# Half-row products and a PSUM bank per head in a windowed attention with two expert layers

## The chip, the cores and the metric

The kernel runs on one core of a Trainium2 chip. The metric is the device time of one execution in microseconds (us). The engines are PE (TensorE: matrix products and transposes), DVE (VectorE), ACT (ScalarE), POOL (GpSimd) and SP (SyncE, which only issues DMA transfers). Each works through its own queue in program order and waits for the others by semaphores. A matrix product reads both operands from SBUF, with the summed index along the partitions, and writes one of eight banks of PSUM, each 128 partitions of 512 fp32 numbers; DVE and ACT read PSUM, POOL doesn't.

## The reference

Attention over 4 batches, 8 heads, 576 positions and 64 numbers per head comes first. Heads 0 to 3 ("plain") see a window of 32 positions, heads 4 to 7 ("dilated") every fourth position of the last 128. Its output, 2304 rows of 512 numbers, passes a layer of eight experts with one chosen per row and a skip score, and then a gated layer.

```
scores = (q @ k.T) / sqrt(64)              # per batch and head, 576 x 576
rel    = i - j
plain:   0 <= rel < 32                     # heads 0..3
dilated: 0 <= rel < 128 and rel % 4 == 0   # heads 4..7
attn   = exp(where(mask, scores, -1e9) - max); attn /= sum + 1e-9
x      = attn @ v                          # -> 2304 x 512
rows with x @ w_skip > 0: x += p * (relu(x @ w1[e]) @ w2[e]),  e = argmax(x @ w_gate), p its softmax weight
out    = (sigmoid(x @ w_gate2) * (x @ w_val)) @ w_out
```

## The kernel before, in words

**Tiles.** The attention is cut into 40 tiles (batch, kind, j): four batches, plain (kind 0) and dilated (kind 1), and five tiles of up to 128 positions (the last plain tile has 64). A batch and kind are a unit of five tiles with four heads. The dilated heads sort their positions by the remainder modulo 4, so that a dilated tile, too, has four groups c of 32 positions with a window of 64 keys each. In a tile a head has the number 2m + h2. K and V hold the two heads h2 of a pair m one above the other: h2 = 0 in partitions 0 to 63, h2 = 1 in 64 to 127.

**Zero blocks.** `kT` keeps, for each pair, one block of columns per head; the half of the partitions that belongs to the other head is zero there. A product over all 128 partitions with q of both heads thus gives each head's scores in its own columns. `vp` and `vd`, the values with windows of 64 keys in 64 partitions per head, have zero blocks in the same way; `vp` has a 65th column of ones, which sums the weights. All zeros are written once, in `setup` (L78) and `clear_dil` (L118): L100 and L101 on DVE, L102 to L104 and L114 to L116 on POOL, L123 on ACT. The same function writes the masks, small bf16 copies on DVE (L105 to L111).

**The work on a tile.** `stage_s` (L244) lays the mask (0 or -1e30) into a bank with one product by the identity (L248) and adds the scores by eight products of 32 queries and 2 x 64 columns, each on one of four groups of 32 columns of PE (`tile_position`, L260); DVE takes the maximum (L265). `stage_e` subtracts it (DVE, L272) and takes the exponential (ACT, L274). `stage_pt` turns the weights (PE, L286) and copies them (L291 or L289). `stage_pv` multiplies by the values in eight products of 130 or 128 columns (L307, L312). `stage_z`, `stage_z1`, `stage_r` and `stage_x` make the sum (L326, dilated tiles only), add 1e-9 (L334), take the reciprocal (L338) and scale (L358), all on DVE; `stage_x` stores the result by one or four DMAs.

**PSUM.** Scores have two banks (`ps_s`), turned weights one (`ps_p`), outputs two (`ps_o`), transposes and logits two (`ps_t`), routing one (`ps_r`); a tile of scores or outputs fills one bank.

**The order of a step.** `attention_phase` (L448) writes the order by hand. Step s issues the scores of tile s, the exponential of s, the turning of s-1, the values of s-2 and the scaling of s-3. `take` puts in the transposes of q and k for the next unit (`tr_plain` L209, `tr_dil` L226), whose PSUM results ACT copies (L242; some of the first on DVE, L240), and releases loads of later q and k. `stage_gate` turns finished rows of x (L383), and `stage_logits` (eight products on 32 columns each, L417, K of 128) and L428 make the routing logits a step later. `todo` places the routing of a batch and `shift_v` (L189: copies each window's second half of V to its first half's partitions; on DVE for the first unit, else on POOL). `keep_busy` issues products that nothing reads (L1619). Loads of the experts' weights (L918) go out on SP between those of V. After the loop the last three tiles are finished, the routing ends, and the expert layer and the gated layer follow; none of those is changed.

The order of one step, as the loop writes it:

```
att.stage_s(*tiles[s])
if s >= 3: att.stage_z(*tiles[s - 3])
run(s, 0, 1); take()            # logits of a gate; a transpose
att.stage_e()
if s >= 3: att.stage_z1()
run(s, 0)
att.stage_pt(*tiles[s - 1])
if s >= 3: att.stage_r(); att.stage_x(*tiles[s - 3])
att.stage_pv(*tiles[s - 2])
```

Of the kernel before, what the change touches and what calls it, by code (L numbers as in the profile page):

```python
# [28 lines left out]
class Attention:  # L29
# [6 lines left out]

    def __init__(self, nc, tc, ctx, g, q, k, v, w_skip, w_gate, xd):
# [40 lines left out]
    def setup(self):  # L78
# [45 lines left out]

    def setup_late(self):
        self.clear_dil(1)
# [29 lines left out]
    def load_v(self, b, kind, between=None):  # L156

        nc = self.nc
        for m in range(2):
            for h2 in range(2):  # L160
                src = self.v[b, 4 * kind + 2 * m + h2]
                p1 = 64 * h2 + W
                if kind == 0:
                    nc.sync.dma_start(
                        out=self.vp[p1:p1 + W, 0:18, m, h2, 0:D],
                        in_=src.rearrange("(c p) d -> p c d", p=W),
                    )
                else:
                    vv = self.vd[:, :, m, h2].rearrange("p j r d -> p j (r d)")
# [9 lines left out]
    def shift_v(self, kind, m, h2, eng):  # L179

        p0, p1 = 64 * h2, 64 * h2 + W
        if kind == 0:
            to, of = self.vp[p0:p1, 1:18, m, h2, 0:D], self.vp[p1:p1 + W, 0:17, m, h2, 0:D]
        else:
            to, of = (
                t.rearrange("p j r d -> p j (r d)")
                for t in (self.vd[p0:p1, 1:5, m, h2], self.vd[p1:p1 + W, 0:4, m, h2])
            )
# [15 lines left out]
    def tr_plain(self, b, nm, c):  # L204
# [6 lines left out]
        for h2 in range(2):  # L211
            for jj in range(2):
# [3 lines left out]
                else:  # L216
                    dst = self.kT[0][64 * h2:64 * h2 + 64, :, h2, W + lo + jj:W + hi:2]
                self.evac(dst, src)

    def tr_dil(self, b, nm, c, m):  # L220
# [7 lines left out]
        for h2 in range(2):  # L228
            for jj in range(2):
# [3 lines left out]
                else:  # L233
                    dst = self.kT[1][64 * h2:64 * h2 + 64, m, h2, jj:4:2, W + lo:W + hi]
# [8 lines left out]

    def stage_s(self, b, kind, j):  # L244
        nc = self.nc
        s = self.bank(self.ps_s, "s", "ps_s", 4, 2 * W)
        mask = self.masks[0 if j else 1 + kind]
        nc.tensor.matmul(  # L248
            s.rearrange("p h t -> p (h t)"), lhsT=self.identb, rhs=mask.rearrange("p h t -> p (h t)"),
            start=True, stop=False, skip_group_check=True,  # L250
        )
        for m in range(2):
            for c in range(2 if (j == 4 and kind == 0) else 4):
                if kind == 0:
                    t0 = 128 * j + W * c
                    lhsT, rhs = self.qT[0][:, m, t0:t0 + W], self.kT[0][:, m, :, t0:t0 + 2 * W]
                else:
                    t0 = W * j
                    lhsT, rhs = self.qT[1][:, m, c, t0:t0 + W], self.kT[1][:, m, :, c, t0:t0 + 2 * W]
                nc.tensor.matmul(  # L260
# [187 lines left out]
def attention_phase(att, route, extra):  # L448
# [47 lines left out]
    for s in range(n):  # L496
# [8 lines left out]
        if s >= 3:  # L505
            att.stage_z(*tiles[s - 3])
# [4 lines left out]
        if s >= 3:  # L511
            att.stage_z1()
# [1193 lines left out]
```

## Time and profile before

| | us |
|---|---|
| three runs | 778.4, 781.0, 784.0 |
| median | 781.0 |
| the profiled execution | 783.2 |
| its span, first to last instruction | 781.5 |
| PE busy | 733.2 (94%) |
| DVE busy | 419.9 (54%) |
| ACT busy | 306.9 (39%) |
| POOL busy | 141.3 (18%) |

The busy shares are those of the span. An engine is busy while it executes; the time in which it waits or issues a transfer is not counted. Ends of PE's products are modelled, and a following product begins before the one ahead of it ends. The timeline merges instructions of a line that follow one another: start, duration, engine, line, operation, tiles, shape, count, and in brackets the idle time before it and what ended it. An fp32 product appears as two instructions.

### The profile page before, as it was taken

The numbers are of one execution on the slowest core, as the hardware profiler recorded it, in microseconds if no ns is written. First come the engines' busy times: TensorE is split into PE (matmuls) and PEld (weight loads), VectorE is DVE, ScalarE is ACT, GpSimd is POOL, SyncE is SP. The second block draws the span as 40 slices with busy tenths as digits, with TensorE's granted clock in tenths as the row PEclk, the third lists the DMA queues.
The fourth block names the chain that finished last, engine by engine and source line by source line (L and its number), as shares of the span: only waits on it lengthen the run. The fifth ranks groups of instructions, "written<-read, shape, count | busy, mean of one in ns | idle before, by whom it ended". The sixth has DMA issues, their size and how long they took to land.

```text
span 781.5 us, 13025 instructions
## 1 busy us (share of the span) xinstructions
PE 733.2 (94%) x4976; PEld 594.7 (76%) x4976; DVE 419.9 (54%) x880; ACT 306.9 (39%) x677; POOL 141.3 (18%) x163
## 2 busy tenths in 40 slices
PE   5999988779999779999999999999999999999995
PEld 3666665568988778978888888888888888888884
DVE  8767767556777757332234546534652653332332
ACT  4888884234545544333352323313321331111110
POOL 7224332312343233100011002000110010000000
PEclk9999999899999989999999999999999999999999
DMA  8799879595597762321012103100310000000122
GB/s 151 166 211 218 226 168 309 162 348 199 184 332 255 264 231 65 117 81 55 1 32 76 28 27 96 40 27 22 87 28 27 28 1 0 1 1 27 55 81 85
DMA packets 74997, 88.12 MB, mean 113 GB/s; under 512 B 15810, under 2 KB 52930, under 8 KB 74912
## 3 DMA queue, kind: packets, MB, share of 16 engines
q1 hardware_dynamic: 71008, 78.68, 34.9%
q0 software_dynamic: 2560, 6.15, 2.2%
q10 hardware_dynamic: 1344, 2.10, 0.7%
q8 instruction: 60, 0.98, 0.5%
q14 instruction: 25, 0.20, 0.1%
HBM read 75.52 MB, written 13.63 MB: 114 GB/s over the span
## 4 chain that ended last, share of the span: by engine, by line
PE 78%; DVE 7%; ACT 6%; DMA 5%; issue 3%; POOL 0%; SPq 0%; DVEq 0%; ACTq 0%; POOLq 0%
PE bank L942 26%; PE bank L947 13%; PE bank L935 8%; PE bank L933 8%; PE bank L934 8%; PE bank L1165 6%; DMA cv_raw<-in_moe_w_val_dram 2%; DMA cv_raw<-in_moe_w_gate_dram 2%; DVE w_lo L928 1%; ACT qTd L242 1%; PE ps_s L260 1%; ACT kTp L242 1%; ACT kTd L242 1%; PE ps_t L383 1%; DVE hl L1211 1%
## 5 line engine op out<-in xcount | busy, mean ns | idle before, releaser
L942 PE MATMUL bank<-fxh,w_hi 128*128 128x512 f32 (+1 forms) x480 | 177.7, 376 | 0.7 <-ACT fxh L1333 0.7
L942 PE MATMUL bank<-fxh,w_lo 128*128 128x512 f32 (+1 forms) x480 | 174.7, 370 | 0.0
L1359 DVE SCALAR_TENSOR_TENSOR th<-th,bank 128x512 f32<-128x512 f32 (+1 forms) x60 | 38.0, 634 | 184.3 <-PE bank L947 161.8
L947 PE MATMUL bank<-fxl,w_hi 128*128 128x512 f32 (+1 forms) x480 | 121.2, 372 | 0.0
L942 PEld LDWEIGHTS bank<-fxh,w_hi 128*128 128x128 f32 x480 | 90.3, 188 | 19.7 <-ACT fxh L1333 1.3
L1007 POOL TENSOR_TENSOR cv_x<-cv_x,cv_s 128x512 f32<-128x512 f32 x36 | 47.6, 1326 | 307.5 <-DVE cv_x L1046 282.2
L942 PEld LDWEIGHTS bank<-fxh,w_lo 128*128 128x128 f32 x480 | 90.3, 188 | 16.1
L947 PEld LDWEIGHTS bank<-fxl,w_hi 128*128 128x128 f32 x480 | 85.6, 188 | 17.5
L1165 PE MATMUL bank<-xt,w 128*128 128x128 f32 (+3 forms) x512 | 74.6, 309 | 16.6 <-issue 9.4
L1360 ACT CAST gh<-th 128x512 fp32r<-128x512 f32 (+1 forms) x60 | 34.7, 578 | 135.3 <-DVE th L1359 135.3
L1165 PEld LDWEIGHTS bank<-xt,w 128*128 128x128 f32 x512 | 71.8, 210 | 19.4 <-issue 9.6
L933 PE MATMUL bank<-w_hi,gh 128*128 128x512 f32 x216 | 85.6, 396 | 0.0
L934 PE MATMUL bank<-w_lo,gh 128*128 128x512 f32 x216 | 85.2, 395 | 0.0
L935 PE MATMUL bank<-w_hi,gl 128*128 128x512 f32 x216 | 85.2, 394 | 0.0
L1358 ACT ACTIVATE th<-bank 128x512 f32<-128x512 f32 (+1 forms) x60 | 33.3, 555 | 127.3 <-PE bank L947 126.8
L1375 DVE SCALAR_TENSOR_TENSOR fo<-bank,fo 128x512 f32<-128x512 f32 x90 | 61.6, 687 | 5.1 <-PE bank L935 3.0
L1361 DVE TENSOR_TENSOR gl<-th,gh 128x512 fp32r<-128x512 f32 (+1 forms) x60 | 39.2, 653 | 38.6 <-ACT gh L1360 38.6
L935 PEld LDWEIGHTS bank<-w_hi,gl 128*128 128x128 f32 x216 | 40.5, 188 | 9.6
L933 PEld LDWEIGHTS bank<-w_hi,gh 128*128 128x128 f32 x216 | 40.7, 188 | 9.2
L934 PEld LDWEIGHTS bank<-w_lo,gh 128*128 128x128 f32 x216 | 40.6, 188 | 9.1
L1002 ACT ACTIVATE cv_x<-cv_raw 128x512 f32<-128x512 f32 x36 | 24.2, 674 | 57.4 <-issue 32.8
L928 DVE TENSOR_TENSOR w_lo<-w,w_hi 128x1024 fp32r<-128x1024 f32 x32 | 41.3, 1292 | 3.7 <-ACT w_hi L927 3.4
(215 smaller groups left out, 1052.8 us busy)
## 6 DMA issues: line engine op xcount, KB each, us to landing
w<-in_moe_w_dram SPq DMA_DIRECT2D x62, 512.0 KB, 6.7
cv_raw<-in_moe_w_val_dram SPq DMA_DIRECT2D x12, 512.0 KB
cv_raw<-in_moe_w_out_dram SPq DMA_DIRECT2D x12, 512.0 KB, 7.1
cv_raw<-in_moe_w_gate_dram SPq DMA_DIRECT2D x10, 512.0 KB, 3.9
out_dram<-fo SPq DMA_DIRECT2D x18, 256.0 KB, 2.0
fx<-xd SPq DMA_DIRECT2D x16, 256.0 KB, 3.0
kp<-in_k_dram SPq DMA_DIRECT2D x12, 192.0 KB, 4.1
qp<-in_q_dram SPq DMA_DIRECT2D x12, 192.0 KB, 5.2
```

What stands on the lines that cost most here:

```text
L928: self.nc.vector.tensor_tensor(out=lo, in0=raw, in1=hi.bitcast(F32), op=ALU.subtract)
L933: nc.tensor.matmul(out, lhsT=lh[0], rhs=rh[0], start=first, stop=False)
L934: nc.tensor.matmul(out, lhsT=lh[0], rhs=rh[1], start=False, stop=False)
L935: nc.tensor.matmul(out, lhsT=lh[1], rhs=rh[0], start=False, stop=last)
L942: nc.tensor.matmul(out, lhsT=lh[a][:, k], rhs=rh[0][:, k], start=first and k + a == k0, stop=False, skip_group_check=True,)
L947: nc.tensor.matmul(out, lhsT=lh[0][:, k], rhs=rh[1][:, k], start=False, stop=last and k == k1 - 1, skip_group_check=True)
L1007: nc.gpsimd.tensor_tensor(out=self.x[i], in0=self.x[i], in1=self.s.pop(i), op=ALU.mult)
L1165: nc.tensor.matmul(ps[:, a, 0:n], lhsT=wt.one[4 * e + c][:, k, 128 * a:128 * a + 128], rhs=xt[:, k, 0:n], start=(k == 0), stop=(k == 3),)
L1359: nc.vector.scalar_tensor_tensor(out=th, in0=th, scalar=1.0, in1=ps[1], op0=ALU.add, op1=ALU.mult)
L1360: nc.scalar.copy(out=hi, in_=th)
L1361: nc.vector.tensor_tensor(out=lo, in0=th, in1=hi.bitcast(F32), op=ALU.subtract)
L1375: nc.vector.scalar_tensor_tensor(out=o, in0=ps, scalar=0.5, in1=o, op0=ALU.mult, op1=ALU.add)
```

## The change

Each product of scores or values now uses only the 64 partitions of its head, on the upper or lower half of PE's rows, and writes a PSUM bank of its head, since both halves may write at one time. K and V lose the zero blocks, and the instructions that wrote them go. Scores and outputs fill two banks each and keep one buffer (`ps_s`, `ps_o`). The mask takes one product per bank. The sum, reciprocal and scaling of tile s-3 move ahead of the scores of tile s. At the end of the attention the scaling of the third last tile comes earlier, and some banks are borrowed from other pools. The reads on DVE get a fourth dimension of access, with the same numbers of elements.

```diff
-        self.ps_s = pool("ps_s", 2, space=PSUM)
+        self.ps_s = pool("ps_s", 1, space=PSUM)
...
-        self.ps_o = pool("ps_o", 2, space=PSUM)
+        self.ps_o = pool("ps_o", 1, space=PSUM)
...
-            big.tile([128, 2, 2, W + S], F32, name="kTp"),
-            big.tile([128, 2, 2, 4, W + 160], F32, name="kTd"),
-        )
-        self.vp = big.tile([128, 18, 2, 2, D + 1], F32, name="vp")
-        self.vd = big.tile([128, NJ, 2, 2, 4, D], F32, name="vd")
+            big.tile([128, 2, W + S], F32, name="kTp"),
+            big.tile([128, 2, 4, W + 160], F32, name="kTd"),
+        )
+        self.vp = big.tile([128, 18, 2, D + 1], F32, name="vp")
+        self.vd = big.tile([128, NJ, 2, 4, D], F32, name="vd")
...
-        self.clear_dil(0)
+        ve.memset(self.kT[0][:, :, 0:W], 0.0)
+        ve.memset(self.vp[:, :, :, D:D + 1], 1.0)
         for h2 in range(2):
-            lo, hi = 64 * h2, 64 * h2 + 64
-            ve.memset(self.kT[0][lo:hi, :, 1 - h2], 0.0)
-            ve.memset(self.kT[0][lo:hi, :, h2, 0:W], 0.0)
-            gp.memset(self.vp[lo:lo + W, 0:1, :, h2, 0:D], 0.0)
-            gp.memset(self.vp[lo:hi, :, :, 1 - h2], 0.0)
-            gp.memset(self.vp[lo:hi, :, :, h2, D:D + 1], 1.0)
+            gp.memset(self.vp[64 * h2:64 * h2 + W, 0:1, :, 0:D], 0.0)
...
-            gp.memset(self.vd[lo:lo + W, 0:1, :, h2], 0.0)
-            gp.memset(self.vd[lo + W:hi, 4:5, :, h2], 0.0)
-            gp.memset(self.vd[lo:hi, :, :, 1 - h2], 0.0)
-
-    def clear_dil(self, h2):
-        lo, hi = 64 * h2, 64 * h2 + 64
+            gp.memset(self.vd[lo:lo + W, 0:1], 0.0)
+            gp.memset(self.vd[lo + W:hi, 4:5], 0.0)
         for m in range(2):
-            k = self.kT[1][lo:hi, m]
-            for block in (k[:, 1 - h2], k[:, h2, :, 0:W], k[:, h2, :, W + 144:]):
-                self.nc.scalar.copy(out=block, in_=self.zero[lo:hi].unsqueeze(2).to_broadcast(list(block.shape)))
+            k = self.kT[1][:, m]
+            for block in (k[:, :, 0:W], k[:, :, W + 144:]):
+                self.nc.scalar.copy(out=block, in_=self.zero.unsqueeze(2).to_broadcast(list(block.shape)))
 
     def setup_late(self):
-        self.clear_dil(1)
...
+    def heads(self, pool, tag, name, n):
+
+        t = pool.tile([128, 2, 512], F32, tag=tag, name=name)
+        return t[:, :, 0:2 * n].rearrange("p h (m t) -> p h m t", m=2)
...
-        s = self.bank(self.ps_s, "s", "ps_s", 4, 2 * W)
+        s = self.heads(self.ps_s, "s", "ps_s", 2 * W)
         mask = self.masks[0 if j else 1 + kind]
-        nc.tensor.matmul(
-            s.rearrange("p h t -> p (h t)"), lhsT=self.identb, rhs=mask.rearrange("p h t -> p (h t)"),
-            start=True, stop=False, skip_group_check=True,
-        )
+        for h2 in range(2):
+            nc.tensor.matmul(
+                s[:, h2], lhsT=self.identb, rhs=mask[:, 0:2], start=True, stop=False, skip_group_check=True
+            )
         for m in range(2):
             for c in range(2 if (j == 4 and kind == 0) else 4):
...
+                for h2 in range(2):
+                    p = slice(64 * h2, 64 * h2 + 64)
+                    if kind == 0:
+                        t0 = 128 * j + W * c
+                        lhsT, rhs = self.qT[0][p, m, t0:t0 + W], self.kT[0][p, m, t0:t0 + 2 * W]
...
+                    nc.tensor.matmul(
+                        s[32 * c:32 * c + 32, h2, m], lhsT=lhsT, rhs=rhs,
+                        start=False, stop=True, skip_group_check=True, tile_position=(64 * h2, 32 * c),
+                    )
...
+                for h2 in range(2):
+                    p = slice(64 * h2, 64 * h2 + 64)
+                    oc = o[32 * c:32 * c + 32, h2, m]
+                    if kind == 0:
+                        rhs = self.vp[p, 4 * j + c, m]
+                    else:
+                        oc, rhs = oc[:, 0:D], self.vd[p, j, m, c]
                     nc.tensor.matmul(
-                        oc, lhsT=lhsT, rhs=self.vp[:, 4 * j + c, m], start=True, stop=True,
-                        skip_group_check=True, tile_position=(0, 32 * c),
+                        oc, lhsT=pt[p, m, 32 * c:32 * c + 32], rhs=rhs, start=True, stop=True,
+                        skip_group_check=True, tile_position=(64 * h2, 32 * c),
                     )
...
-        att.stage_s(*tiles[s])
         if s >= 3:
             att.stage_z(*tiles[s - 3])
+            att.stage_z1()
+            att.stage_r()
+            att.stage_x(*tiles[s - 3])
+        att.stage_s(*tiles[s])
         run(s, 0, 1)
...
         att.stage_e()
-        if s >= 3:
-            att.stage_z1()
...
-        if s >= 3:
-            att.stage_r()
-            att.stage_x(*tiles[s - 3])
-            if tiles[s - 3][1] == 1:
-                gates.append(tiles[s - 3][::2])
+        if s >= 3 and tiles[s - 3][1] == 1:
+            gates.append(tiles[s - 3][::2])
...
-    att.stage_pv(*last[1])
+    x(last[0])
+    att.stage_pv(*last[1], (att.ps_s, "s", "ps_s"))
...
-    att.stage_pv(*last[2], (att.ps_p, "pt", "ps_p"))
+    att.stage_pv(*last[2])
```

## Rows read from the trace of the kernel before

**Rows 1.** Stages: us; busy (count) of PE, PEld, DVE, ACT, POOL; clock; DMA, GB/s

```profile
24.32:132.66 108.34, 99.40 (x1678) 67.76 (x1677) 79.58 (x294) 86.64 (x288) 37.60 (x61) 0.98 0.89 213
...
150.00:182.00 32.00, 24.71 (x157) 22.68 (x158) 15.08 (x18) 11.23 (x16) 6.66 (x7) 0.89 0.94 318
182.00:781.00 599.00, 579.87 (x2874) 486.43 (x2873) 292.97 (x464) 191.60 (x324) 78.73 (x62) 0.99 0.24 80
```

**Rows 2.** The same view, cut into steps: 8, 12, 15, 35, 37, 38

```profile
37.53:40.73 3.20, 2.68 (x45) 1.72 (x44) 1.99 (x7) 3.06 (x10) 0.00 (x0) 1.00 1.07 178
...
49.76:52.64 2.88, 2.88 (x55) 2.19 (x55) 2.17 (x9) 2.32 (x9) 0.00 (x0) 1.00 0.52 128
...
58.65:60.95 2.30, 2.30 (x46) 1.61 (x44) 1.40 (x7) 2.18 (x9) 1.04 (x1) 1.00 0.95 258
...
119.23:120.97 1.74, 1.74 (x37) 1.05 (x36) 1.48 (x6) 0.25 (x1) 0.77 (x1) 1.00 1.15 274
...
122.82:126.93 4.11, 2.31 (x44) 1.27 (x42) 3.87 (x15) 1.48 (x5) 2.33 (x4) 0.95 1.03 287
126.93:129.88 2.95, 2.95 (x41) 1.57 (x38) 1.79 (x9) 0.38 (x2) 1.71 (x8) 0.50 0.98 310
```

**Rows 3.** Timeline of DVE, 0 to 15 us

```profile
1.43 1.07 DVE L100 MEMSET kTp<- 64x1216 f32 x1 [0.20 <-issue]
...
4.58 3.00 DVE L107 COPY mask<-mask 32x256 bf16<-32x256 bf16 x3
...
10.62 1.40 DVE L240 COPY qTp<-ps_t 64x192 f32<-64x192 f32 x4
...
14.44 0.43 DVE L265 TENSOR_REDUCE mx<-ps_s 128x4 f32<-128x256 f32 x1
```

**Rows 4.** Timeline of POOL, 0 to 16 us

```profile
4.67 2.06 POOL L103 MEMSET vp<- 64x2340 f32 x1
...
6.97 0.54 POOL L114 MEMSET vd<- 32x512 f32 x1
```

**Rows 5.** Timeline of PE, 0 to 26 us

```profile
5.14 0.85 PE L209 MATMUL ps_t<-ident,qp 96*128 96x96 f32 x4
6.77 1.01 PE L1619 MATMUL ps_t<-r_one 128*128 128x512 bf16 x2 [0.78 <-ACT kTp L242]
...
12.07 1.08 PE L260 MATMUL ps_s<-kTp,qTp 128*32 128x128 f32 x16 [3.25 <-DVE qTp L240]
```

**Rows 6.** Timeline of SP, then DMA issues with KB and us to landing

```profile
3.85 4.11 SPq L164 DMA_DIRECT2D vp<-in_v_dram  x4
...
vp<-in_v_dram SPq DMA_DIRECT2D x4, 144.0 KB, 5.8
```

**Rows 7.** Timeline of PE in step 12

```profile
49.76 0.27 PE L248 MATMUL ps_s<-mask,identb 128*128 128x256 bf16 x1
49.96 0.65 PE L260 MATMUL ps_s<-kTp,qTp 128*32 128x128 f32 x16
50.42 0.40 PE L417 MATMUL ps_l<-xt,w 128*32 128x128 f32 x8
...
51.12 0.65 PE L307 MATMUL ps_o<-vp,pt 128*32 128x130 f32 x16
51.71 0.66 PE L383 MATMUL ps_t<-ident,x 128*128 128x128 f32 x4
```

**Rows 8.** Timeline of PE, logits of the last tiles

```profile
138.13 0.43 PE L417 MATMUL ps_l<-xt,w 128*32 128x128 f32 x8
...
138.81 0.32 PE L417 MATMUL ps_l<-xt,w 128*32 128x64 f32 x8
```

**Rows 9.** Timeline of DVE in step 12

```profile
50.67 0.42 DVE L265 TENSOR_REDUCE mx<-ps_s 128x4 f32<-128x256 f32 x1 [0.56 <-PE ps_s L260]
...
51.34 0.41 DVE L272 TENSOR_TENSOR sb<-ps_s,mx 128x256 f32<-128x256 f32 x1
...
52.27 0.42 DVE L358 TENSOR_TENSOR x<-ps_o,z 128x256 f32<-128x256 f32 x1
```

More of the change, by code (lines that the diff above doesn't have):

```diff
@@ L182, in shift_v @@
         if kind == 0:
[L183 removed]
+            to, of = self.vp[p0:p1, 1:18, m, 0:D], self.vp[p1:p1 + W, 0:17, m, 0:D]
         else:
@@ L186, in shift_v @@
                 t.rearrange("p j r d -> p j (r d)")
-                for t in (self.vd[p0:p1, 1:5, m, h2], self.vd[p1:p1 + W, 0:4, m, h2])
+                for t in (self.vd[p0:p1, 1:5, m], self.vd[p1:p1 + W, 0:4, m])
             )
@@ L252, in stage_s @@
         for m in range(2):
             for c in range(2 if (j == 4 and kind == 0) else 4):
[L254 to L260, printed above, removed]
-                    s[32 * c:32 * c + 32, 2 * m:2 * m + 2, :], lhsT=lhsT, rhs=rhs,
-                    start=False, stop=True, skip_group_check=True, tile_position=(0, 32 * c),
-                )
+                for h2 in range(2):
[4 more added lines that the diff above has]
+                    else:
+                        t0 = W * j
+                        lhsT, rhs = self.qT[1][p, m, c, t0:t0 + W], self.kT[1][p, m, c, t0:t0 + 2 * W]
+                    nc.tensor.matmul(
+                        s[32 * c:32 * c + 32, h2, m], lhsT=lhsT, rhs=rhs,
+                        start=False, stop=True, skip_group_check=True, tile_position=(64 * h2, 32 * c),
+                    )
@@ L299, in stage_pv @@
                 self.X[b, j // 2] = self.xw.tile([128, 2, 2, 256], F32, tag="x", name="x")
-        o = self.bank(*(place or (self.ps_o, "o", "ps_o")), 4, D + 1)
+        o = self.heads(*(place or (self.ps_o, "o", "ps_o")), D + 1)
         nv = 2 if (j == 4 and kind == 0) else 4
@@ L303, in stage_pv @@
             for c in range(nv):
-                lhsT = pt[:, m, 32 * c:32 * c + 32]
-                oc = o[32 * c:32 * c + 32, 2 * m:2 * m + 2]
-                if kind == 0:
+                for h2 in range(2):
[3 more added lines that the diff above has]
+                        rhs = self.vp[p, 4 * j + c, m]
+                    else:
+                        oc, rhs = oc[:, 0:D], self.vd[p, j, m, c]
                     nc.tensor.matmul(
-                        oc, lhsT=lhsT, rhs=self.vp[:, 4 * j + c, m], start=True, stop=True,
-                        skip_group_check=True, tile_position=(0, 32 * c),
-                    )
-                else:
-                    nc.tensor.matmul(
-                        oc[:, :, 0:D], lhsT=lhsT, rhs=self.vd[:, j, m, :, c], start=True, stop=True,
-                        skip_group_check=True, tile_position=(0, 32 * c),
-                    )
+                        oc, lhsT=pt[p, m, 32 * c:32 * c + 32], rhs=rhs, start=True, stop=True,
+                        skip_group_check=True, tile_position=(64 * h2, 32 * c),
+                    )
+        o = o.rearrange("p h m t -> p m h t")
         self.O[b, kind, j] = o
@@ L322, in stage_z @@
         if kind == 0:
-            zs = self.O[b, kind, j][0:n, :, D:D + 1]
+            zs = self.O[b, kind, j][0:n, :, :, D:D + 1]
         else:
@@ L333, in stage_z1 @@
         n, zs, z = self.ZS
-        self.nc.vector.tensor_scalar(out=z[0:n], in0=zs, scalar1=1.0e-9, scalar2=None, op0=ALU.add)
+        out, zs = z[0:n], zs[0:n]
+        if len(zs.shape) == 4:
+            out = out.rearrange("p (m h) o -> p m h o", h=2)
+        self.nc.vector.tensor_scalar(out=out, in0=zs, scalar1=1.0e-9, scalar2=None, op0=ALU.add)
     def stage_r(self):
@@ L559, in attention_phase @@
     att.stage_gate(*gates[0])
-    att.stage_pv(*last[1])
+    x(last[0])
+    att.stage_pv(*last[1], (att.ps_s, "s", "ps_s"))
     xts = {j: att.xt_tile(b, j) for j in range(2, NJ)}
-    ps = [att.bank(att.ps_s, "s", "ps_s", 4, 128) for _ in range(2)]
+    ps = [att.bank(att.ps_t, "t", "ps_t", 4, 128) for _ in range(2)]
     halves = {2: ps[0][:, 0:2], 3: ps[0][:, 2:4], 4: ps[1][:, 0:2]}
@@ L571, in attention_phase @@
     for j, t in zip(range(2, NJ), last):
-        x(t)
-        ps = att.bank(*((att.ps_t, "t", "ps_t") if j < 4 else (att.ps_s, "s", "ps_s")), 2, 128)
+        if j > 2:
+            x(t)
+        ps = att.bank(*((att.ps_t, "t", "ps_t") if j < 4 else (att.ps_p, "pt", "ps_p")), 2, 128)
         att.turn(ps, b, j, 1)
```

19 lines of the change are left out of this document (11 added, 8 removed).

## The prediction

> **What bounds the kernel now.** I read the busy time by stage first [rows 1]: attention's steps, 24.3 to 132.7 us, then the routing, the first experts, and 599 us that are one stretch of products. From 182 us on PE is busy 580 of 599 us and nothing in that stretch is touched, so the change can only move the moment at which it begins. Between 150 and 182 us PE idles 7 us while DMA is busy 0.94 of the time; those weight loads are let go by the experts' own progress, so this stretch moves as a whole with its beginning.
>
> Next I cut the attention into its 40 steps, each from one mask product to the next [rows 2]. Four kinds show. PE has no idle time in the steps that also turn the finished rows and make logits (2.88 busy of 2.88), of which there are ten: 10 to 13, 20 to 23, 30 and 34. It has none either in 3, 4, 15, 16, 25 and 26, but ACT is close behind (2.18 of 2.30). In thirteen steps ACT is the limit (3.06 of 3.20): 5 to 9, 17 to 19, 27 to 29, 31 to 33. The last five are mixed, with DVE and PE in turn.
>
> The first steps are another matter. The first score products start at 12.07 us, after PE has waited 3.25 us for DVE's copies of q [rows 5], and the first maximum runs at 14.44 [rows 3]. DVE gets there late because of preparation: two memsets of 1.07 that clear K's zero blocks, then three small mask copies that take 3.00 in all [rows 3]. Those copies are short by themselves; the first of them runs while POOL clears zero blocks of V in one instruction of 2.06 us, from 4.67 to 6.73 [rows 4], and ends only then.
>
> **The change, part by part.** *Preparation.* Gone are DVE's two K memsets (2.1 us), POOL's two 2.06 us memsets of V, its two larger ones of the dilated V and most of what ACT clears. Left on POOL are two short memsets, some 0.2 each, and four of 0.54 [rows 4]. They begin at 2.2 as now and end near 4.9 us (2.2 + 0.4 + 4 x 0.54), and no mask copy can be held longer than one of them. With 0.54 for each of five copies and 0.17 for two memsets, DVE is done near 5.4 us, instead of 10.6. The next limit is q's transposition, which waits for its load and ends at 5.14 + 0.85 = 6.0 us [rows 5]. The four copies of q take 1.40 [rows 3]: 7.4. PE's two filler products wait for the copies of K on ACT and end at 6.77 + 1.01 = 7.8 [rows 5]; the mask product follows, so the scores start near 8.2 instead of 12.07. They take 1.08 there now, not the 0.65 of later steps; with 0.75, if the new form helps, the first maximum runs at 9.0 (else at 9.3) instead of 14.44: **-5.4 us**. From there I leave the chain as it is, with DVE's same instructions in the same order, but for 0.2 that the second score stage gives: **-5.6**. The cover that could be gone is V: its first load is issued at 3.85 and lands after 5.8 [rows 6], at 9.65, and DVE's shifting copy of it wants it near 9.9. Bounds: -3.9 (only the start of the scores counts) to -6.2.
>
> *Scores and values.* Eight products of 128 columns on all rows become sixteen of 64 columns, half of them on the other half of the rows; every fp32 product is two instructions, so 16 become 32. In the rows [rows 7] 16 instructions take 0.65; the last starts 0.38 after the first (one lasts 0.27). The rows that resemble the new form are the logits of a short tile, 64 columns: eight take 0.32 against 0.43 for eight of 128 [rows 8]. Four column groups run beside one another, a round of four takes 0.11 at 128 columns ((0.65 - 0.43)/2) and half of that, 0.055, at 64. If the row halves also run beside one another, a round holds eight instructions, and four rounds end: the last start is 0.10 (two rounds, the short row's) + 2 x 0.055 + 0.03 = 0.24 after the first, and it lasts 0.27 - 0.055 = 0.22: 0.46 instead of 0.65, **-0.19 per stage**. If they don't, there are eight rounds of 0.055 and nothing is won. If an instruction can't start faster than the 16 do now (0.38/15 = 25 ns), 32 of them need 0.78 to the last start: +0.35. No row shows two halves at once; I take -0.19, because in the short row eight start within 0.10, 14 ns apart, so 25 ns isn't a floor.
>
> *Mask.* One product of 256 columns becomes two of 128. From it to the scores 0.20 pass now [rows 7]; the second adds 0 to 0.20, and I take 0.07, since both stream half as much.
>
> *The change of tiling between scores and logits.* Now the logits follow the scores at the pace of a round (0.46 from first to first), while the turning product that follows the values starts 0.59 after them [rows 7]: a change of form of the array costs 0.13. The new scores use half rows, the logits don't, so this may come in at that place too: 0 to 0.13, taken at 0.13. [...] No row of this trace shows a change between these two forms.
>
> Per step PE thus gets shorter by 0.19 + 0.19 - 0.07 = 0.31, and by 0.18 where logits follow.
>
> *What the steps make of it.* Ten steps with logits, PE the limit: 10 x 0.18 = 1.8. Six with ACT 0.12 behind: 0.7. Steps 35 and 36, DVE right behind (1.48 of 1.74 [rows 2]): 0.4. Steps 38 and 39, the former at half clock: 0.7. Steps 14 and 24, ACT and PE in turn: 0.2. The thirteen ACT steps and 37: 0. Together **-3.8**; 0 if halves don't overlap. After the last step two value stages stay in PE's chain: **-0.4**.
>
> *The new order and single buffers.* Sum, reciprocal and scaling of tile s-3 go ahead of the scores of tile s on DVE, because both score and output tiles now fill two banks and have one buffer. The scaling takes 0.42 [rows 9], and the three others together less than twice that, so 1.2 at most, in a time in which DVE waits today for the scores (0.56 before the maximum [rows 9]); the maximum stands behind them, and ACT's exponential behind that. The scores of step s+1 must wait for the subtraction of step s, and behind a waiting mask product stands all of PE's step: the subtraction ends at 51.75 and the next mask product begins the next step at 52.64 [rows 2, 9], 0.9 later. The value product of tile s-2 waits for the scaling of s-3, which is now queued half a step ahead of it. On SP the scaled rows' stores (one, or four in the dilated units) are moved past the loads of k and q that the same step may release; these are wanted a unit later, so 0. Cost of it all 0, up to 0.3 in the steps in which DVE works on routing, 17, 27 and 37 (3.87 of 4.11 [rows 2]).
>
> *Loads.* DMA is busy 0.89 of 108 us, 96 us of work that doesn't shrink [rows 1]; the steps would take 104. Late loads of V take back 0 to 3.8; I take **+0.8**.
>
> Sum: -5.6 - 3.8 - 0.4 + 0.8 = -9.0. The profiled execution took 783.2 us (781.5 of span and 1.7 around it), 2.2 above the median of 781.0, within the runs' spread. From 783.2 the sum gives 774.2; from the median 772.0, which I forecast.
>
> **The rivals.**
> - *The halves take turns on PE.* For it: no row shows otherwise. Against: the column groups do run beside one another. Then S and V gain nothing, the mask (0.07) and the drain (0.13) remain: in the twenty steps with PE at the limit 10 x 0.2 + 10 x 0.07 = +2.7. With the start: -2.9, **778**.
> - *The steps' gain is hidden* behind ACT and the loads, and only the start counts: -5.6 + 0.5 = **776**. For it: ACT within 0.12 of the limit in many steps, DMA 0.89.
> [...]
> - *Slower: starting instructions becomes PE's limit.* Place: scores and values of each step. At 25 ns between starts a stage grows by 0.35, a step by 0.8 with mask and drain; the twenty steps with PE at the limit pay +16, the ACT steps, which hide 0.4, +5: with the start's -5.6, **796**. It decides from some 16 ns: there 31 x 16 = 0.50 to the last start, 0.06 over today's pace per stage (0.44), 0.27 a step with mask and drain, x 20 = 5.4, the start's gain. [...] The short logits, 14 ns apart on average, disagree already [rows 8].
>
> **How the numbers follow.** Forecast 0.56; turns 0.14; hidden 0.14; clock 0.08; slower 0.08. About 1%, 7.8 us, is what a measurement of this kernel can tell. The forecast's own range is 768 to 775 (start -3.9 to -6.2, steps -2.5 to -5); a little of it is above 773.2. Faster by over 1%: 0.56; within 1%: 0.35; slower by over 1%: 0.09. The range reaches to the rivals without the slow one: 767 to 780.5.
>
> **What would show it.** Right: the first maximum near 9 us; mask copies under 0.6 each; 32 instructions in about 0.46 in scores and values; steps with logits near 2.7; PE's 599 us stretch unchanged and 9 us earlier. Wrong: a stage of 0.65 or more; the clock at 0.50 within the steps; DVE waiting for V at 10 us; idle PE before mask or value products with DVE named; the first expert not earlier although the steps are.

## The result and the profile after

The changed kernel took 792.1 us, the median of four runs (789.55 to 794.56), beside 781.1 (778.4 to 784.0) for the kernel before: ratio 1.0141 [1.0108, 1.0175]. It is slower by 1.4%, and the forecast of 772.0 with its range up to 780.5 missed it. The profiled execution took 794.56, with a span of 792.8 against 781.5.

The attention's last mask product (step 39) begins at 141.12 us instead of 129.88. From there to the end pass 651.7 us, and 651.6 before. So in these two executions all of the 11 us was lost in the attention's steps. The stages, as in [rows 1] (us; busy time and count of PE, of PEld, which is PE's loading of weights, of DVE, ACT and POOL; mean granted clock as a share of full speed; DMA share, GB/s):

```profile
17.71:141.12 123.41, 104.25 (x2763) 74.13 (x2761) 81.91 (x287) 85.04 (x284) 37.68 (x61) 0.78 0.81 200
161.00:194.00 33.00, 27.28 (x168) 24.65 (x167) 15.45 (x23) 11.79 (x16) 6.31 (x7) 0.84 0.82 272
194.00:792.00 598.00, 577.33 (x2871) 484.09 (x2869) 293.82 (x464) 191.51 (x324) 80.78 (x63) 0.99 0.25 83
```

The first row holds steps 3 to 38. They began 6.6 us earlier than before (17.71 against 24.32) and took 123.4 us. PE is idle for 19 of these and the mean clock is 0.78. Before, the same steps took 105.6 us, with PE idle for 8.6 and the clock at 0.98:

```profile
24.32:129.88 105.56, 97.00 (x1639) 66.28 (x1638) 77.27 (x285) 85.62 (x285) 37.60 (x61) 0.98 0.88 208
```

The small predictions came right. On DVE the three mask copies take 1.02 instead of 3.00, and the first maximum runs at 7.86 instead of 14.44 [rows 3]:

```profile
2.24 1.02 DVE L104 COPY mask<-mask 32x256 bf16<-32x256 bf16 x3 [0.42 <-POOL mask L92]
...
7.86 0.42 DVE L265 TENSOR_REDUCE mx<-ps_s 128x4 f32<-128x256 f32 x1
```

On PE, step 12 at the full clock, to be laid beside [rows 7]: 32 score instructions in 0.45 and 32 value instructions in 0.46, where 16 took 0.65; 0.39 from the scores to the logits. What was costed at nothing is in the fourth row: the value product waits for the scaling x, because there is one output buffer.

```profile
46.71 0.27 PE L246 MATMUL ps_s<-mask,identb 128*128 128x128 bf16 x2
46.91 0.45 PE L259 MATMUL ps_s<-kTp,qTp 64*32 64x64 f32 x32
47.30 0.43 PE L423 MATMUL ps_l<-xt,w 128*32 128x128 f32 x8
...
48.32 0.46 PE L314 MATMUL ps_o<-vp,pt 64*32 64x65 f32 x32 [0.23 <-DVE x L364]
```

The next rows are steps 8, 12, 15, 20, 21 and 35, cut as in [rows 2] and with the columns of the first rows above. Step 8 takes 2.28 instead of 3.20 and step 15 takes 1.98 instead of 2.30, but step 12 is no shorter. Steps 20, 21 and 35 are where it goes wrong: 8.66, 4.73 and 4.53 us, at clocks of 0.50 to 0.78.

```profile
35.46:37.74 2.28, 2.13 (x79) 1.61 (x77) 2.04 (x7) 2.16 (x8) 0.00 (x0) 1.00 1.07 230
46.71:49.65 2.94, 2.71 (x89) 1.99 (x89) 2.35 (x8) 2.21 (x9) 0.00 (x0) 1.00 0.38 94
55.22:57.20 1.98, 1.98 (x78) 1.48 (x77) 1.64 (x7) 1.86 (x8) 1.04 (x1) 1.00 1.00 256
69.17:77.83 8.66, 4.92 (x93) 3.60 (x90) 2.75 (x9) 2.69 (x10) 4.42 (x4) 0.70 0.85 197
77.83:82.56 4.73, 4.73 (x91) 3.48 (x92) 2.55 (x9) 2.31 (x9) 0.04 (x1) 0.50 0.60 142
...
128.05:132.58 4.53, 1.95 (x69) 1.21 (x69) 2.07 (x9) 1.07 (x3) 1.93 (x4) 0.78 0.90 247
```

**The pauses.** The timeline of PE in step 20 shows the first cause. After 11 of 32 score instructions PE stops for 3.74 us, in the middle of a stage whose data are all there; "issue" means that it waits for nothing that the profile shows:

```profile
69.38 0.32 PE L259 MATMUL ps_s<-kTp,qTp 64*32 64x64 f32 x11
73.44 0.64 PE L259 MATMUL ps_s<-kTp,qTp 64*32 64x64 f32 x21 [3.74 <-issue]
```

PE's waits from 17.71 to 141.12 us, in sum, times and longest, put 11.9 us on such pauses. The same view of the kernel before, 24.32 to 129.88 us, has no such row.

```profile
PE ps_s L259 <- issue: 6.2, 3, 3.7
PE ps_o L314 <- issue: 3.8, 2, 2.3
...
PE ps_r L816 <- issue: 1.4, 1, 1.4
...
PE ps_t L218 <- issue: 0.5, 1, 0.5
```

Count all of PE's instructions from its first: the products, the weight loads, and the semaphore waits and branches between them. Then the pauses stand at the 450th, 706th, 3010th, 4034th, 4290th, 5570th and 5826th, always a multiple of 256 apart. The page's DMA queues name what comes in such pieces. In the whole execution the queue q8, of kind "instruction", moves 1.15 MB in 70 packets, 16 KB each, against 0.98 MB in 60 before; the kernel has 15545 instructions instead of 13025. That q8 carries PE's program is read from the counts: in steps 3 to 38 it brings 21 packets where PE has some 5500 products and weight loads, and 13 before, where it has some 3300. First after, then before:

```profile
q8 instruction: 21, 0.34, 1.3%
```

```profile
q8 instruction: 13, 0.21, 1.0%
```

The DMA queues in two stretches around the pause (packets, MB, share of the 16 engines) show when the piece came. First 64.0 to 70.9 us, in which PE runs into the block's end at 69.7; then 70.9 to 72.1:

```profile
q1 hardware_dynamic: 2220, 1.36, 93.3%
q14 instruction: 1, 0.01, 0.5%
```

```profile
q1 hardware_dynamic: 904, 0.23, 88.0%
q8 instruction: 1, 0.02, 5.3%
```

PE entered the block before this one at 64.3. For the next 6.6 us the queue of loads and stores (q1) has the DMA engines, and no block of PE's program (q8) comes. Then one comes (70.95 to 71.96), and PE goes on 1.5 us after it; at the other pauses it goes on 1.2 to 1.6 us after such a packet has landed. The steps before used up a block in 8.1 us (13 in the 105.6 us of steps 3 to 38); the new steps go through the same work with 21 blocks. Before, too, a packet set out only 0.1 to 4.4 us after PE had entered the block ahead of it, but each had landed at least 2.2 us before PE needed it. So the ends of these blocks cost PE no wait, and the one in the changed kernel's step 20 cost 3.74 us.

**The clock.** The second cause, in windows of steps 2 to 29 (columns as above): low from 11.7 to 35.5 us, although PE was busy 22.73 of 23.76, low again for some 13.7 us behind the pauses of steps 20 and 26, and for 17 us behind that of step 35 (from 130.6 to 147.7). Before, the steps were at full speed from step 3 on, and one drop later lasted about a step (0.50 in step 38 [rows 2]).

```profile
11.70:35.46 23.76, 22.73 (x457) 16.82 (x457) 16.46 (x45) 16.44 (x54) 4.13 (x4) 0.51 0.88 180
35.46:69.17 33.71, 28.75 (x930) 20.84 (x929) 27.59 (x97) 29.30 (x97) 11.10 (x19) 1.00 0.86 209
73.44:86.80 13.36, 13.36 (x256) 9.79 (x257) 6.75 (x22) 5.67 (x20) 5.29 (x5) 0.52 0.73 182
86.80:96.50 9.70, 7.68 (x250) 5.47 (x250) 6.85 (x26) 8.60 (x32) 2.67 (x5) 1.00 0.90 247
96.92:110.70 13.78, 12.42 (x270) 9.12 (x271) 8.78 (x32) 9.18 (x28) 5.74 (x13) 0.52 0.78 158
```

So three theories were to be tested. Theory 1: the doubled instruction count uses up blocks faster than they come through the loads. Theory 2: half-row products leave the clock low after a drop. Theory 3, a rival: the new order on DVE and the single buffers cost it.

### The profile page after: what moved, and what is told of

The parts are those of the page before. It is cut to its first block, busy times and chain, and to the rows that moved or that the text cites. A ratio compares the mean times of both kernels' runs of the same rounds, so it can differ in the third digit from the quotient of the medians.

```text
span 792.8 us, 15545 instructions
## 1 busy us (share of the span) xinstructions
PE 737.6 (93%) x6232; PEld 601.5 (76%) x6232; DVE 417.4 (53%) x878; ACT 302.5 (38%) x669; POOL 132.3 (17%) x157
## 3 DMA queue, kind: packets, MB, share of 16 engines
q8 instruction: 70, 1.15, 0.6%
## 4 chain that ended last, share of the span: by engine, by line
PE 78%; DMA 6%; DVE 5%; ACT 5%; issue 4%; SPq 0%; POOL 0%; POOLq 0%; DVEq 0%; ACTq 0%
PE bank L948 25%; PE bank L953 12%; PE bank L941 8%; PE bank L939 8%; PE bank L940 8%; PE bank L1171 4%; DMA xd<-xg,r_dst 2%; PE ps_o L314 2%; PE ps_s L259 2%; PE ps_p L289 1%; PE ps_t L218 1%; DMA xg<-xd,r_src 1%; DVE w_lo L934 1%; PE ps_t L389 1%; PE ps_t L201 1%
## 5 line engine op out<-in xcount | busy, mean ns | idle before, releaser
L1171 PE MATMUL bank<-xt,w 128*128 128x128 f32 (+3 forms) x512 | 71.7, 303 | 16.2 <-DVE hl L1217 9.2
L1171 PEld LDWEIGHTS bank<-xt,w 128*128 128x128 f32 x512 | 69.5, 205 | 18.3 <-DVE hl L1217 9.7
L934 DVE TENSOR_TENSOR w_lo<-w,w_hi 128x1024 fp32r<-128x1024 f32 x32 | 39.1, 1221 | 3.1 <-ACT w_hi L933 2.7
```

The source lines that it names most:

```text
L934: self.nc.vector.tensor_tensor(out=lo, in0=raw, in1=hi.bitcast(F32), op=ALU.subtract)
L1171: nc.tensor.matmul(ps[:, a, 0:n], lhsT=wt.one[4 * e + c][:, k, 128 * a:128 * a + 128], rhs=xt[:, k, 0:n], start=(k == 0), stop=(k == 3),)
```

## The experiments

Medians of the kernel before in the four groups of runs: 780.95 (e1 to e4), 779.8 (e5 to e8), 780.2 (e9 to e12), 779.6 (e13 to e16). Each kernel has one profile. In that of the kernel before the last mask product comes at 129.88 us; in those of e4, e5, e9, e10, e12 and e14 to e16, whose medians lie within 0.6% of it, at 125.0 to 129.9 (e6's, of the slowest of its ten executions, has it at 133.8). So a difference of under 5 us at this place says nothing by itself.

**e1, the count alone.** The kernel before, with 32 tiny products of zeros ahead of each tile's scores (64 more instructions a tile, as the change adds):

```diff
+        for i in range(32):
+            c = i % 4
+            nc.tensor.matmul(
+                s[32 * c:32 * c + 32, 0, 0:8], lhsT=self.g.one[:, 0:32], rhs=self.g.zero[:, 0:8],
...
```

> The kernel before, with 32 tiny products (a load of 32 columns, 8 columns streamed, all zeros, on the four column groups) after each mask product: 64 more PE instructions per tile, as many as the change adds, and no other part of it. Theory 1 (blocks of instructions: PE's program comes in blocks of 256 instructions by DMA, and a program that uses a block up sooner meets a late block): idle time of 1 to 4 us in the middle of stages, at PE instructions 256 apart, 8 to 15 us of it in sum, the clock at 0.50 for 10 us and more after it, and a time of 790 to 800. Theory 2 (the half-row products keep too little of PE active, and the clock falls by itself): only the time of the tiny products, 0.2 to 0.4 us in the twenty steps with PE at the limit: 784 to 789, no pauses, clock near 0.98. Theory 3 (the single buffers and the new order make PE wait): as theory 2.

801.1 us, ratio 1.0251 [1.0214, 1.0288], a little above the 790 to 800 expected. The pauses are there, in a kernel with full-row products, and again multiples of 256 instructions apart; the longest rows of PE's waits from 24 to 148 us:

```profile
PE ps_s L266 <- issue: 4.4, 2, 3.3
PE ps_s L254 <- issue: 4.4, 2, 3.7
PE ps_s L248 <- issue: 2.1, 1, 2.1
```

12.7 us in all with two shorter rows, against 11.9. Theory 1 holds. A side effect has a share in the total: the first tiny products wait for POOL's tile of zeros, and step 1 begins at 17.20 instead of 14.42. The expected 10 us and more of low clock didn't come: it was back 3 to 7 us after it fell, behind each of the three long pauses (windows after the pause that ends at 77.98):

```profile
78.00:81.50 3.50, 3.50 (x34) 1.96 (x38) 2.48 (x9) 0.58 (x2) 1.08 (x1) 0.50 0.76 135
81.50:85.00 3.50, 3.50 (x82) 2.59 (x82) 2.19 (x6) 1.17 (x4) 3.31 (x4) 0.69 0.96 231
85.00:110.00 25.00, 23.77 (x646) 17.92 (x645) 17.49 (x71) 20.69 (x70) 6.79 (x15) 1.00 0.78 202
```

**e2, fewer loads beside the attention.** The changed kernel, its 18 loads of expert weights issued behind the attention instead of one per step:

```diff
-                        wt.load(2 if n < 18 and n // 4 % 2 else 1)
+                        late.append(s)
```

> The changed kernel, with the 18 loads of expert weights that it issues within the attention put behind it. Theory 1: the blocks that were late behind those loads come in time, so the pauses near 132, 138 and 144 us go (they were 2.3, 1.5 and 1.0), the one at 97 (2.2) shrinks, the one at 73 us (3.7, behind loads of q, k and v alone) stays; the last mask product comes at 130 to 136 instead of 141 us. Theory 2 and 3: it stays within 1.5 us of 141. The whole time says little, as the experts then wait for their weights.

Last mask product at 131.46 instead of 141.12. The same instructions, with the DMA share down from 0.81 to 0.61, pause for 7.0 us instead of 11.9; what is left is mostly one wait near 68 us, where k, q and v are still loaded:

```profile
PE ps_t L201 <- issue: 3.6, 1, 3.6
...
PE ps_o L314 <- issue: 1.9, 1, 1.9
```

So the loads beside the attention set how late a block comes. The pauses make up 4.9 of the 9.7 us; the mean clock is also higher, 0.86 instead of 0.78. The lower level, 0.50, lasted 6.8 us behind the pause near 68 and 3.4 behind the one near 104, with the changed kernel's own products. The total, 801.3, says nothing, as the weights come late.

**e3, the first wait filled.** The changed kernel, with eight full-row products of 512 columns ahead of step 1's scores, where PE waits:

```diff
+        for _ in range(FILL.get((b, kind, j), 0)):
+            self.g.ones(t[:, 0].rearrange("p (a c) -> p a c", c=128))
+FILL = {(0, 0, 1): 8}
```

> The changed kernel, with eight products that nothing reads (512 columns, all rows) ahead of the mask product of step 1, where PE waits 2.4 us for the copies of q. If that wait alone let the clock fall at 12 us: full clock from 5 to 73 us, step 8 begins near 31 instead of 35.5, and the time is 787 to 789. If the new products can't hold or bring back the clock: it falls before 25 us all the same and stays low for 10 us and more; the time stays within 2 us of 792.

794.07 us, 1.0173 [1.0135, 1.0212]: nothing gained. The clock was full to step 1's end, fell all the same, and stayed low to 36.7 (window of steps 3 to 7). The first wait alone isn't the cause.

```profile
17.73:36.73 19.00, 16.99 (x351) 12.38 (x350) 11.03 (x34) 13.90 (x46) 4.13 (x4) 0.50 0.78 161
```

**e4, the start's gain without new products.** The kernel before; K's zero blocks cleared by ACT, one mask copy and ACT's second clearing moved behind the first scores, POOL's clearing of the dilated V behind the first steps. In it a part of the dilated V is cleared after its load, so these values are zeros.

```diff
-            ve.memset(self.kT[0][lo:hi, :, 1 - h2], 0.0)
+            nc.scalar.copy(out=k, in_=self.zero[lo:hi].unsqueeze(2).to_broadcast(list(k.shape)))
...
+    at(1, 1, 3, att.setup_md)
+    at(1, 1, 3, att.setup_vd)
```

> The kernel before, products and buffers unchanged, with its preparation put in another order: K's zero blocks by ACT, V's zeros on POOL after the small ones, the dilated mask and the dilated V's zeros in step 1. If the first steps' gain (the first maximum at 7.9 instead of 14.4 us) is worth what the prediction said, the first maximum comes before 8.5 us, every later step some 5 to 6 us earlier, and the time is 775 to 777. If later steps swallow it (loads, clock): 779 to 782.

779.72 us, 0.9986 [0.9962, 1.0011]: no difference. Step 3 did begin 6.5 us earlier (17.85), but in steps 7 and 8 (4.60 and 4.68 us) the values wait for POOL, which now clears at 26 us what must be clear before its copies of V; at step 10 1.9 us of the gain are left.

**e5, order, buffers and tail alone**, with the full-row products and zero blocks of before; **e14** is the same kernel again, on another chip.

```diff
-        self.ps_s = pool("ps_s", 2, space=PSUM)
+        self.ps_s = pool("ps_s", 1, space=PSUM)
...
+            att.stage_z1()
+            att.stage_r()
+            att.stage_x(*tiles[s - 3])
+        att.stage_s(*tiles[s])
```

> The kernel before with the changed kernel's order on VectorE (sums, reciprocal and scaling ahead of the scores), its single buffers of scores and outputs and its tail, but with the full-row products and zero blocks of before. Theory 1 (the doubled PE instructions use up their 256-instruction blocks faster than the DMA queues deliver them): the instruction count is that of before, so no new pauses in mid-stage, 781 to 784 us. Rival (the single buffers and the new order cost it: the value products wait 0.2 to 0.5 us a step for the scaling): 35 steps by 0.3 us, 790 us or more, with no mid-stage pauses.

> The kernel with the changed order, single buffers and tail, but the full-row products of before, run once more: 0.994 of before if the first result was real, 0.998 to 1.001 if it was the chip's scatter.

e5: 775.7 us, 0.9943 [0.9926, 0.9959], five runs. e14: 778.98, 0.9993 [0.9976, 1.0010], twelve runs. The gain didn't repeat; whether the first result was scatter that its interval didn't cover, or belonged to that chip, is open. Neither has an "issue" wait of 0.4 us or more in steps 3 to 38, and neither is slower than before. Theory 3 falls.

**e9, e15, e16, which part of these would have mattered.** e9: the order alone, two buffers each. e15: order and tail, two buffers. e16: order and tail, a single buffer of scores, two of outputs.

> The kernel before with the changed kernel's order on VectorE alone (sums, reciprocal and scaling ahead of the scores' maximum); two buffers of scores and of outputs as before, tail as before. Theory A (the order by itself is what made the kernel with order and single buffers faster by 4 us; its single buffers only cost, 3.65 and 4.03 us in steps 11 and 21): 773 to 776 us. Rival B (the order does nothing, the gain is from the tail or the buffers): 779 to 781.

> The changed order and the changed tail, with the two buffers of scores and outputs of before. If the tail is what gave 4 us: 774 to 777. If single buffers did, or nothing did: 779 to 781.

> The changed order and tail with a single buffer of scores and two of outputs. If the single output buffer only costs (steps 11 and 21 were 0.8 to 1.0 us longer with it): 1 to 2 us less than with single buffers of both, 773 to 775. Rival: the same as before, 779 to 781.

0.9997 [0.9976, 1.0019], 1.0007 [0.9991, 1.0023], 1.0012 [0.9987, 1.0036]: none of them makes a difference.

**e6, e7, half of the new products.** e6: half-row scores, values and V as before. e7: half-row values, scores and K as before (the changed hunks of the other half undone).

```diff
# e6
-        self.vp = big.tile([128, 18, 2, D + 1], F32, name="vp")
+        self.vp = big.tile([128, 18, 2, 2, D + 1], F32, name="vp")
# e7
-            big.tile([128, 2, W + S], F32, name="kTp"),
+            big.tile([128, 2, 2, W + S], F32, name="kTp"),
```

> The changed kernel with the value products of before (128 partitions, zero blocks in V, two buffers of one bank for the outputs); the scores stay half-row. About half of the added PE instructions. Theory 1: about half of the lost time in mid-stage pauses (4 to 7 us of 13), low clock behind them, and the start's gain kept: 783 to 788 us. Rival (each half-row product costs by itself, in the starts or the drain): the score stage 0.46 us for 32 as in the changed kernel, the pauses unchanged, 790 or more.

> The changed kernel with the score products of before (zero blocks in K, K's zeroing back on VectorE and ScalarE, two buffers of one bank for the scores); the values stay half-row. Theory 1: half of the added instructions, half of the pauses, and the start as before (first scores near 12 us): 786 to 791 us. Rival (the scores alone are what costs): 779 to 782.

e6: 781.97, 1.0011 [0.9984, 1.0039]. e7: 787.62, 1.0094 [1.0055, 1.0132]. PE's pauses in the steps, e6 and then e7:

```profile
PE ps_s L262 <- issue: 1.0, 2, 0.6
```

```profile
PE ps_s L266 <- issue: 5.8, 3, 2.7
```

Both add half of the instructions (14316 and 14259 in all). In e7 the three long pauses stand multiples of 256 instructions apart; in e6 the blocks came nearly in time, against the 4 to 7 us of pauses expected, and its one long wait (3.1 us, for a DMA by the profile) stands at no such boundary. The reading that fits both is that the count sets how late a block may come and the loads decide whether it does; why they did so in e7 and hardly in e6 was not looked into.

**e8, full-row work in the low stretches.** The changed kernel, three full-row products of 512 columns ahead of the scores in eight steps:

```diff
+FILL = {t: 3 for t in ((0, 0, 2), (0, 0, 3), (0, 0, 4), (0, 1, 0), (2, 0, 1), (2, 0, 2), (2, 1, 2), (2, 1, 3))}
```

> The changed kernel with three full-row products of 512 columns ahead of the scores in steps 2 to 5, 21, 22, 27 and 28, where its clock was granted at half for 14 to 24 us. Theory 2 (half-row products leave the granted clock low after a drop, full-row ones bring it back): full clock again by 25 us instead of 35.6, and in step 22 and 28 at the latest; step 8 begins near 33 instead of 35.5; 789 to 793 us. Rival (the clock comes back after a fixed time, or only once the pauses are gone, whatever PE does): low until 35 us as before, and the fillers add 24 by 0.43 us: 798 to 805.

More work for PE, and step 8 begins 2.5 us earlier (33.01 against 35.46): the clock is back at 18.7 us instead of 35.5 (windows of step 2 and of steps 3 to 7).

```profile
15.12:18.72 3.60, 3.60 (x80) 2.40 (x79) 3.09 (x9) 1.78 (x6) 0.00 (x0) 0.65 1.14 225
18.72:33.01 14.29, 12.14 (x355) 8.38 (x354) 9.36 (x32) 12.09 (x41) 4.13 (x4) 1.00 0.73 163
```

So far theory 2 holds: full-row work at the start was followed by the full clock. The last mask product came at 133.67, 7.5 earlier, but 4.2 of that are shorter pauses (7.7 us in all instead of 11.9), which the fillers weren't meant to change. The median, 791.5 (1.0182 [1.0128, 1.0236]), hardly moved: in the profiled execution 655.2 us follow the last mask product instead of 651.7, and why is open.

**e12, the same for e6**: half-row scores, fillers in steps 2 to 5.

```diff
+FILL = {t: 3 for t in ((0, 0, 2), (0, 0, 3), (0, 0, 4), (0, 1, 0))}
```

> Half-row scores with the value products of before, and three full-row fillers in each of steps 2 to 5. Theory 2 (full-row work brings the clock back): full clock by 25 us instead of some 36, step 10 about 3 us earlier than 45.0: 777 to 780 us. Rival (value products of full rows are full-row work already, so the fillers only add 12 by 0.21 us): 783 to 785.

780.12, 1.0016 [0.9993, 1.0039]. In the profiles the clock rose sooner: step 5's transposing product (two of 128 columns) takes 0.38 in e12, and 0.63 in e6 at the same time; step 10 begins at 41.65 instead of 44.99. In the medians of e6 and e12 (782.0 and 780.1, ranges 777 to 786 and 778 to 785) it isn't resolved.

**e13, the shape without the count.** The changed kernel with half-row products of the first head alone. The second head's scores are the mask, its values one product of ones.

```diff
-                for h2 in range(2):
+                for h2 in range(1):
...
+        nc.tensor.matmul(
+            o[:, 1], lhsT=self.identb, rhs=ones, start=True, stop=True, skip_group_check=True
+        )
```

> The changed kernel with the half-row products of the first head of each pair alone (8 scores and 8 values a tile instead of 16 and 16); the second head's scores are the mask and its values a single product of ones. So the products have the changed shape, but PE's instruction count is near that of before. Theory 1 (the count makes the pauses): none of the mid-stage pauses of 1 us or more, last mask product at 125 or earlier, 773 to 778 us. Theory 2 (the half-row shape leaves the clock low): the granted clock still low from 11 to some 35 us, no drops later as nothing pauses. Rival (the shape itself makes the pauses): pauses of 2 to 4 us as in the changed kernel, 788 or more.

This run has one cause without the other. 12973 instructions, and no wait "issue" at all in steps 3 to 38, though at the low clock a block also lasts longer (14 blocks in 136.6 us). But the clock is at 0.50 from step 3 to the last, with PE busy all the time (steps 3 to 19; 20 to 38; behind them):

```profile
18.31:81.45 63.14, 63.14 (x781) 46.62 (x782) 40.15 (x128) 43.63 (x142) 18.84 (x27) 0.50 0.81 180
81.45:154.87 73.42, 73.22 (x928) 52.88 (x927) 46.29 (x159) 41.84 (x142) 18.80 (x35) 0.50 0.66 174
154.87:200.00 45.13, 35.45 (x296) 26.99 (x293) 22.59 (x80) 13.43 (x32) 7.28 (x7) 0.73 0.70 210
```

803.9 us, 1.0313 [1.0288, 1.0339]. The number for theory 1 (773 to 778) was missed, as the effect of theory 2 is far stronger than was thought: with one row half at work in scores and values the lower level never ended in the attention; with both, as in the changed kernel, it ended after 14 to 24 us. That it is the half rows is argued: the new products also stream 64 columns instead of 128, and e13 does half of their work. No run parts these.

**e11, both remedies at once**: the changed kernel with e2's late loads, and fillers in steps 2 to 5, 21 and 22.

```diff
+FILL = {t: 3 for t in ((0, 0, 2), (0, 0, 3), (0, 0, 4), (0, 1, 0), (2, 0, 1), (2, 0, 2))}
```

> The changed kernel with full-row fillers in steps 2 to 5, 20 and 21's place, and the expert-weight loads behind the attention. If pauses at the blocks and the low clock after a drop are the whole of what the prediction missed, its attention comes near the forecast: last mask product near 124 (the late loads alone 131.5, the fillers' start 2.5 to 3 earlier, 4 us less low clock behind the pause near 68), against 129.9 before, 141.1 changed. Rival (a third cost in the steps): 128 or later. The total means nothing here, the weights come late: near 795.

Last mask product at 129.44, 11.7 earlier than in the changed kernel, mean clock in the steps 0.98. That is 5 later than expected, and by its number the rival's case. PE's waits still hold 7.2 us of pauses, behind the loads of k, q and v:

```profile
PE ps_s L262 <- issue: 4.6, 5, 1.7
...
PE ps_s L249 <- issue: 1.9, 1, 1.9
...
PE ps_o L317 <- issue: 0.7, 1, 0.7
```

129.44 less 7.2 is 122.2, near the 121.3 of the forecast (129.88 - 5.6 - 3.8 + 0.8) and within the scatter of this place. So no third cost is needed; that there is none was not shown, since the loads of q, k and v can't be taken away.

**e10, a candidate**: the order of e9 and e4's preparation, with all clearing of V ahead of its loads.

```diff
     att.load_v(0, 0)
+    att.setup_vd()
```

> The order of the run before, and the preparation of the earlier run moved as well, with all zeroing of V on GpSimd ahead of V's loads. Theory: the start's gain of the changed kernel (step 3 some 6 us earlier) needs no half-row products; without the 4 us that steps 7 to 9 lost to the late zeroing, 3 to 5 us stay at the last mask product: 769 to 773 us. Rival (GpSimd's zeroing slows VectorE's copies between 8 and 17 us, or what is gained is given back to loads and to the experts' waits): 774 to 777.

779.41, 1.0005 [0.9979, 1.0031]: no difference. The edit puts POOL's clearing beside DVE's copies of V, and two of these take over three times the 0.75 of the third:

```profile
10.03 2.58 DVE L200 COPY vp<-vp 32x1088 f32<-32x1088 f32 x1
...
14.01 2.46 DVE L200 COPY vp<-vp 32x1088 f32<-32x1088 f32 x1
...
17.41 0.75 DVE L200 COPY vp<-vp 32x1088 f32<-32x1088 f32 x1
```

Step 1 takes 8.04 us, and step 3 begins at 21.37. As long as the zero blocks are there, somebody clears them beside the start. No version in this study is repeatably faster than the kernel before.

## Why the prediction was wrong, point by point

- *Preparation, -5.6*: right, even small. Step 3 began 6.6 us earlier. But at 35.46 only 2.1 of it were left, at step 8 (37.53 before): the steps between ran at the lower clock.
- *Scores and values, -0.19 a stage*: right in size, 0.45 and 0.46. The halves run beside each other, 32 instructions in 0.45 where 16 took 0.65; "the halves take turns" and "starting instructions becomes PE's limit" fall. The 32 starts of step 12 lie within 0.24 us, 8 ns apart on average, as the forecast had it; the slower rival was worked out at 25 ns.
- *The change of tiling, 0.13; mask, 0.07*: the logits start 0.39 after the scores, where the forecast gives 0.46 - 0.19 + 0.13 = 0.40, so the first term is borne out in size. The rivals' sums call this 0.13 the drain; no run shows that PE drains there, only the 0.39 from scores to logits. The scores still start 0.20 after the first mask product, so the second costs nothing there.
- *What the steps make of it, -3.8*: too much by half where the clock was full. Steps 9 to 19 took 31.43 us instead of 31.93; by the prediction's list it is 1.06 (4 x 0.18 + 2 x 0.12 + 0.1).
- *New order and single buffers, 0*: near right. The value product waits (0.23 in step 12), but e5, e14 to e16 show no cost in the total.
- *Two value stages after the last step, -0.4*: not seen; 651.7 us follow the last mask product, and 651.6 before.
- *Loads, +0.8*: the right resource with the wrong victim. I looked at late V; late was PE's own program.
- **The step that failed** is "every fp32 product is two instructions, so 16 become 32". The count was priced only by the pace of starts. It also makes PE's program longer, 21 blocks instead of 13 in the steps, and 11.9 us of pauses come from it (e1 shows the count alone to do so; e13, at the lower clock, has the shape without the count and no pause). The page showed what was needed: 60 packets of 16 KB in the instruction queue, and DMA busy 0.89.
- The second is the granted clock. It had a chance of 0.08; "the clock at 0.50 within the steps" stood among the signs of being wrong, and came. In its steps the kernel before had shown one drop, to 0.50 in step 38, behind a step in which PE was busy 2.31 of 4.11 [rows 2]. In the changed kernel it didn't fall in idle ACT steps (1.00 from 35.46 to 69.17, with PE busy 28.75 of 33.71); it fell at the start and at pauses, and with the new products it stayed down for longer (0.50 for 136.6 us in e13; in e8, with full-row work added, back at 18.7 instead of 35.5). The pauses were on no list.

Forecast and result differ by 19.8 us at the last mask product (121.3 against 141.12): 11.9 are pauses; the other 7.9 lie in the low clock, in steps that didn't get shorter, and in scatter of up to 5 us at this place, and were not parted further.

## To carry to other kernels

Price a change that raises an engine's instruction count by the blocks of its program too: packets of the instruction queue over the stretch, beside the DMA share there; of the blocks beside busy load queues here, seven came late in the changed kernel's steps, each behind one that lasted 3.5 to 7.1 us, and none in the steps of before, where a block lasted 7.0 to 9.0. Before splitting products over PE's row halves, look whether the stretch has clock drops: behind the changed kernel's long pauses the lower level lasted 14 to 17 us, against 3 to 7 with full rows (step 38 before, e1); in e2 it was 3 to 7 with the new products too, so what decides is open. And an "issue" wait in the middle of a stage asks for a count of the engine's instructions, waits and branches included: here the long ones were multiples of 256 apart.

## What of the hardware was not expected

- PE's program came in 16 KB packets, one of them more than 6.6 us after the block before it was entered, behind loads at a DMA share of 0.93; PE went on 1.2 to 1.6 us after the late ones had landed. Why the loads go first is open.
- In e13, with scores and values on one row half, the granted clock stayed at 0.50 for 136.6 us in which PE was busy 136.4; in e8, with three full-row products of 512 columns in step 2, it was back at 1.00 before step 3, at 18.7 us.
- Thirty-two half-row instructions started within 0.24 us at the full clock, and took 0.45 where 16 on all rows took 0.65.
- In e10, which puts POOL's clearing beside DVE's copies of V, two of these copies took 2.58 and 2.46 us, and the next two 0.75 each.
